# Down stages of a retention and SwiGLU kernel: both score groups of the first pair in one part, the second group in the banks of later token blocks

## The chip, the cores and the metric

The kernel runs on one core of a Trainium2 chip. The metric is the device time of one execution in microseconds, as a median of several runs. A profiled execution gives a trace as well, with a start and a duration for every instruction of the five engines: TensorE (PE, with its weight loads as PEld), VectorE (DVE), ScalarE (ACT), GpSimd (POOL) and SyncE (SP, which issues most DMAs here).

## The reference

Two blocks follow each other. The first is a recurrent retention over 4 batches, 8 heads, 768 tokens and a head size of 64:

```python
for t in range(S):
    state = gamma[None, :, None, None] * state + np.einsum('bhd,bhe->bhde', k[:, :, t], v[:, :, t])
    y[:, :, t] = scale * np.einsum('bhd,bhde->bhe', q[:, :, t], state)
```

Its output, as 3072 tokens of 512 features, goes through a SwiGLU feed-forward block with 1536 hidden features:

```python
g = x @ w_gate
silu = g * (1.0 / (1.0 + np.exp(-g)))
val = x @ w_val
return (silu * val @ w_out).astype(np.float32)
```

## The kernel before

**Tiling.** The sequence is cut into chunks of 128 tokens, six for each batch. Three chunks of one batch and the three of the same place in the next batch make a segment of 768 tokens, and four segments make the whole. A *pair* is the two chunks, one of each batch, at one place of a segment, so a segment has three pairs, 0 to 2.

**Stages.** For each segment there is an up stage, which makes the hidden features from the attention output, and a down stage, which multiplies them by `w_out`. The first segment's attention and up stage are written out by hand (`START`, `beside`, function `up`, line 695). The later up stages (`up3`, matmuls at line 866) split their operands into three terms. A down stage (line 916) goes over the 12 blocks of 128 hidden features; for each it runs six *token blocks* of 128 tokens, each three matmuls of 128x128 by 128x512, and each token block accumulates in a PSUM bank of its own, 0 to 5, over the whole stage. So a down stage has 72 slots, numbered n = 6f + b. The three terms of a hidden block are made by `h_split`: ScalarE (line 760), VectorE (line 763) and, for the third term, VectorE again (line 80).

**Attention inside a down stage.** The down stages of the first three segments also compute the attention of the next segment. It is cut into parts, which stand between token blocks at fixed slots. For each pair the parts are: scores of group 0, scores of group 1 (a group is four of the eight heads), "m" (own-half mix), "o" (other-half mix) and "t" (new states):

```python
CYCLE = [("s", 0, 0), ("s", 1, 4), ("m", 0, 9), ("o", 0, 12), ("t", 0, 16)]
STARTS = (2, 22, 41)
```

All matmuls of these parts are issued by the helper `mm` (line 551). They are small: they use a quarter of the array (64 by 64), or half of it for the states. The trace has 32 records of matmuls for one scores part, 16 with 128 columns and 16 with 64. `scores_of(p, g)` writes the two halves of a group's scores into banks 6 and 7 (`R0` is 6). `decayed` (line 570) then multiplies each half by its mask on VectorE and puts it into one of four places of `tmp`. `scale_q2` multiplies the pair's q in place by a decay (one chunk on VectorE, line 80, and one on GpSimd, line 624), where the next segment is not at the start of a sequence. It needs both groups' scores to have read q.

**Order of work.** Nothing is decided while the kernel runs. Every piece is put into a list with a planned time (`at(t, fn)`), the list is sorted by that time, and each engine and DMA queue gets its instructions in that order. The planned times (`WHEN`, `COST`, `PASS_D`) thus set only the order. Waits between engines are added by the framework from the tiles that instructions read and write. Each engine and queue works in order, so an instruction that waits holds those behind it.

**Around the change.** In the first down stage the last gate products of the up stage (`last_gates`, with results at lines 710 and 711) come after the first token block, and the first round of token blocks has its own order, (0, 4, 3, 2, 5, 1). In the others the order is 0 to 5. Ahead of the second and third down stage, `up3` uses banks 0 to 3, 6 and 7. SP's queue brings later pairs' k, q and v (`load_pair`, line 545) and the blocks of `w_out` (`w_load`, line 909), in planned order.

Of the kernel before, what the change touches and what calls it, by code (L numbers as in the profile page):

```python
# [17 lines left out]
P = 128  # L18
B, H, S, D = 4, 8, 768, 64
# [13 lines left out]
TA = 3 * P  # L33
# [16 lines left out]
def tile_retnet_swiglu(  # L50
# [22 lines left out]
    add, mul, sub = ALU.add, ALU.mult, ALU.subtract  # L73
    tt, stt, pool = (nc.vector.tensor_tensor, nc.vector.scalar_tensor_tensor,
                     nc.gpsimd.tensor_tensor)
# [39 lines left out]
    banks = [psum.tile([P, 512], F32, name=f"bank{i}") for i in range(8)]  # L115
# [4 lines left out]
    def at(t, fn, *args, **kw):  # L120
        events.append((t, len(events), lambda: fn(*args, **kw)))
# [23 lines left out]
    def seg_chunks(s):  # L145
        p, pos = divmod(s * L, NCK)
        return [(2 * p + i) * NCK + pos + j for j in range(L) for i in range(2)]
# [144 lines left out]
    def do(order):  # L292
# [40 lines left out]
    WHEN = {  # L333
        ('u', 0): (1.15, 2.16, 2.86, 3.39, 4.9, 5.3, 8.05, 13.63, 7.4, 8.1),
        ('u', 1): (0.41, 2.51, 3.16, 3.92, 4.38, 5.59, 6.95, 8.3, 7.26, 12.66),
        ('u', 2): (0.33, 1.32, 3.61, 3.15, 4.0, 5.51, 5.85, 6.13, 7.28, 7.66),
        ('u', 3): (1.63, 1.81, 3.34, 2.86, 3.53, 5.07, 6.18, 7.14, 7.05, 7.54),
        ('w', 0, 0): (-11.39, -6.27, -4.75),
        ('w', 0, 1): (-7.89, -7.84, -1.53),
        ('w', 0, 2): (-10.42, -10.31, -9.95),  # L340
        ('w', 1, 0): (-9.1, -4.79, -3.1),
# [71 lines left out]
    att = {}  # L413
    first_chunks = seg_chunks(0)

    def pairs(t):
        return t.rearrange("p (n t) -> p n t", n=NP)
# [84 lines left out]
    def mix(c):  # L502
        vn, a = chunks[c][2], att.pop(c)
        y, own = y_parts(c)
        for k, (n, i, to) in enumerate(own):
# [11 lines left out]
    side = [t.rearrange("p (i t) -> p i t", i=2)  # L517
            for t in (tab[:, : 2 * TA], kept_vk.rearrange("p a b -> p (a b)")[:, : 2 * TA])]
    kdec_b = tab[:, ds(2 * TA, H)]
    half = [ds(0, D), ds(D, D)]  # L520
    given = {}
    R0 = 6
# [27 lines left out]
    def mm(o, a, b, start=False):  # L550
        nc.tensor.matmul(o, a, b, start=start, stop=True, skip_group_check=True)  # L551

    def scores_of(p, g):
        kt, qt = ([pairs(t) for t in given[p][w]] for w in range(2))
        for b in range(2):
            for m in range(2):
                for r in range(2):
                    x, n = half[r], 2 * g + b
                    mm(banks[R0 + r][half[m], ts(b, P)], kt[m][x, n, half[0]],
                       qt[m][x, n], b == 0)  # L560
        for b in range(2):
            for m in range(2):
                for r in range(2):
                    x, n = half[r], 2 * g + b
                    mm(banks[R0 + r][half[m], ds(2 * P + D * b, D)],
                       kt[1 - m][x, n, half[1]], qt[1 - m][x, n, half[1]])

    def decayed(p, g, i):
        att[p, g, i] = tmp[:, ts(2 * g + i, TA)]
        tt(att[p, g, i], banks[R0 + i][:, :TA], side[g][:, i], op=mul)  # L570

    def y_both(h, i, c):
        return banks[R0 + c].rearrange("p (i b t) -> p i b t", i=2, b=2)[half[h], i]
# [245 lines left out]
    def make_x(t, s, p):  # L819
        for m, d in enumerate(WHEN["sum", p]):  # L820
            at(t + d, sum_x, m)
        for n in range(3):
            for d, step in zip(WHEN["far", p, n], (
                    lambda n=n: far_a(*x_part(s, p, n)), lambda n=n: far_b(*x_part(s, p, n)),
                    lambda n=n: far_c(x_part(s, p, n)[0]), lambda n=n: far_d(x_part(s, p, n)[0]))):
                at(t + d, step)
# [66 lines left out]
    def h_split(t, f, when):  # L893
        it = {}

        def begin():
            hs[f] = item("g", 2 * TH)
            it["o"] = [hs[f][:, i] for i in range(3)]
            near_a(it["o"], hT[:, f].rearrange("p i t -> p (i t)"))

        a, b, c = WHEN["h", when]
        at(t + a, begin)
        at(t + b, lambda: near_b(it["o"], hT[:, f].rearrange("p i t -> p (i t)")))
        at(t + c, lambda: near_c(it["o"], both))

    def w_load(t, f):
        def load():
            wo[f] = item("o", DM)
            nc.sync.dma_start(out=wo[f].bitcast(U32), in_=w_dn3[f])

        at(t - 8.0, load)
# [25 lines left out]
        nc.sync.dma_start(out=out[ds(row, P)], in_=t)  # L937


    CYCLE = [("s", 0, 0), ("s", 1, 4), ("m", 0, 9), ("o", 0, 12), ("t", 0, 16)]  # L940
    STARTS = (2, 22, 41)
    PARTS = {}
    for p, b in enumerate(STARTS):
        for what, g, n in CYCLE:
            PARTS[b + n] = what, p, g
    COST = {"s": 1.0, "m": 1.3, "o": 1.1, "t": 0.8}
    LOADS = {5: 7, 6: 15, 7: 19, 8: 19, 9: 27, 10: 39, 11: 46}
    UNITS = (40, 59, 62)

    def down_stage(s, t, first_order=range(6), between=None):  # L950
        nxt = s + 1 if s + 1 < NSEG else None
        slot_at, steps = [], []
        for n in range(6 * NF):
            f, b = divmod(n, 6)
            slot_at.append(t)
            if b == 0:
                steps.append(t)
            if nxt and n in PARTS:
                what, p, g = PARTS[n]
                ci = seg_chunks(nxt)[2 * p] % NCK  # L960
                d = t + COST[what] + 0.1
                if what == "s":
                    at(t, scores_of, p, g)
                    w = WHEN["s", p, g]
                    for i in range(2):
                        at(d + w[i], decayed, p, g, i)
                    if g and ci:
                        for i in range(2):
                            at(d + w[2 + i], scale_q2, p, i)
                elif what == "m":  # L970
                    at(t, mix_own, nxt, p)
                    w = WHEN["m", p]
                    at(d + w[0], fence)
                    if ci < NCK - 1:
                        for i in range(2):
                            at(d + w[1 + i], scale_k2, p, i)
                elif what == "o":
                    at(t, mix_other, nxt, p)
                    if p == 0:
                        at(t, begin_x, nxt)  # L980
                    for k, w in enumerate(WHEN["y", p]):
                        at(d + w, bring_y, k % 2, k // 2 % 2, k // 4)
                    if ci < NCK - 1:
                        at(d + WHEN["old", p], decay2, nxt, p)
                    make_x(d, nxt, p)
                elif ci < NCK - 1:
                    at(t, state2, nxt, p)
                    at(d + WHEN["new", p], keep_state, nxt, p)
                t += COST[what]
            tok = (first_order if f == 0 else range(6))[b]  # L990
            at(t, down, f, tok)
            t += 3 * PASS_D
            if f == NF - 1:
                at(t + WHEN["end" if nxt else "last"][tok], finish, s, tok)
            if between and n == 0:
                at(t, between)
                t += 1.0
        for f in range(NF):
            h_split(steps[f], f, f if nxt else NF)
            if s or f > 2:  # L1000
                w_load(steps[f], f)
        if nxt:
            for n, h in LOADS.items():
                at(slot_at[h] + 1.0, load_pair, nxt, n)
            for f in range(3):
                at(slot_at[UNITS[f]], load_unit, f)
        return t
# [24 lines left out]
    end = T0 + NF * UP0  # L1032
# [4 lines left out]
    at(end, do, beside[-1])  # L1037
    for n in range(3, 5):
        at(end + 1.0 + n, load_pair, 1, n)
    t = down_stage(0, end, (0, 4, 3, 2, 5, 1), last_gates)  # L1040
    for s in range(1, NSEG):
        for f in range(NF):
            up3(s, f, t + UPT * f)
            if f > 2:
                at(t + UPT * (f - 1) - 2.5, load_unit, f)
        t += NF * UPT
        if s + 1 < NSEG:
            for n in range(5):
                at(t - (18, 13, 12, 5, 4)[n], load_pair, s + 1, n)
        t = down_stage(s, t)  # L1050
# [52 lines left out]
```

## Time and profile before

| | |
|---|---|
| median of 3 runs | 669.22 us (667.5 to 669.8) |
| profiled execution | 669.52 us |
| its span, first to last instruction | 667.7 us |
| TensorE busy | 655.4 us, 98% of the span |
| VectorE, ScalarE, GpSimd busy | 463.1, 386.2, 252.0 us |
| granted TensorE clock | 1.000 |
| chain that ended last | 82% TensorE, 8% DMA, 3% VectorE |

Rows of the timeline give the start in us, the duration of the group in us, engine, line, operation, what it writes and reads, the shape, the count, and in brackets how long the engine had been idle and what ended the idle time. "issue" there means that no wait on another engine is recorded. Rows of the chain of waits give start, duration and what was on the chain. PE records overlap their neighbours a little, and their ends are modelled, so the chain, which has no overlaps, is the better ruler for TensorE.

### The profile page before, as it was taken

The numbers are of one execution on the slowest core, as the hardware profiler recorded it, in microseconds if no ns is written. First come the engines' busy times: TensorE is split into PE (matmuls) and PEld (weight loads), VectorE is DVE, ScalarE is ACT, GpSimd is POOL, SyncE is SP. The second block draws the span as 40 slices with busy tenths as digits, with TensorE's granted clock in tenths as the row PEclk, the third lists the DMA queues.
The fourth block names the chain that finished last, engine by engine and source line by source line (L and its number), as shares of the span: only waits on it lengthen the run. The fifth ranks groups of instructions, "written<-read, shape, count | busy, mean of one in ns | idle before, by whom it ended". The sixth has DMA issues, their size and how long they took to land.

```text
span 667.7 us, 12348 instructions
## 1 busy us (share of the span) xinstructions
PE 655.4 (98%) x4712; PEld 547.5 (82%) x4712; DVE 463.1 (69%) x742; ACT 386.2 (58%) x792; POOL 252.0 (38%) x165
## 2 busy tenths in 40 slices
PE   8998999999999999999999999999999999999997
PEld 7754555567778999997777999998777999999885
DVE  3667988887778767675778666667766776668541
ACT  2687887755737555555648655555574655654111
POOL 1444657730104655640111655661000656652000
PEclk9999999999999999999999999999999999999999
DMA  8799799877665533455674534365766444323553
GB/s 325 268 388 340 250 402 393 334 261 237 226 214 218 197 110 129 169 176 206 238 251 168 206 111 145 112 210 180 240 216 228 161 177 151 111 89 110 188 189 142
DMA packets 48459, 141.32 MB, mean 212 GB/s; under 512 B 4752, under 2 KB 17808, under 8 KB 48400
## 3 DMA queue, kind: packets, MB, share of 16 engines
q1 hardware_dynamic: 47968, 139.88, 59.7%
q8 instruction: 37, 0.61, 0.4%
q10 hardware_dynamic: 432, 0.66, 0.3%
q14 instruction: 22, 0.18, 0.1%
HBM read 113.78 MB, written 26.74 MB: 210 GB/s over the span
## 4 chain that ended last, share of the span: by engine, by line
PE 82%; DMA 8%; DVE 3%; ACT 2%; issue 2%; SPq 1%; POOL 1%; ACTq 0%; POOLq 0%; DVEq 0%
PE bank L866 39%; PE bank L916 29%; PE bank L695 6%; PE bank L551 6%; DMA rawp<-in_w_gate_dram 2%; DMA loads<-in_w_out_dram 1%; DMA oitem<-wdnt 1%; DMA tab<-in_decays_dram 1%; DMA wdnt<-oitem 1%; SPq L194 1%; DMA hT<-in_q_t_dram 1%; POOL first L237 1%; ACT bank L221 1%; DVE first L231 0%; ACT chunk_x L801 0%
## 5 line engine op out<-in xcount | busy, mean ns | idle before, releaser
L866 PE MATMUL bank<-x,gitem 128*128 128x384 f32 x1296 | 231.5, 335 | 0.0
L866 PEld LDWEIGHTS bank<-x,gitem 128*128 128x128 f32 x1296 | 226.0, 188 | 0.5
L916 PE MATMUL bank<-oitem,gitem 128*128 128x512 f32 x864 | 215.1, 401 | 0.6 <-DMA oitem<-wdnt 0.4
L916 PEld LDWEIGHTS bank<-oitem,gitem 128*128 128x128 f32 x864 | 158.7, 188 | 41.5 <-issue 2.9
L766 POOL TENSOR_TENSOR gitem<-gitem 128x768 fp32r<-128x768 f32 x72 | 138.5, 1946 | 114.7 <-DVE gitem L763 110.3
L695 PE MATMUL bank<-first 128*128 128x384 f32 x336 | 110.8, 489 | 2.8 <-ACT tmp L716 1.4
L695 PEld LDWEIGHTS bank<-first 128*128 128x128 f32 x336 | 62.9, 190 | 48.8 <-ACT tmp L732 2.6
L760 ACT ACTIVATE gitem<-loads 128x768 fp32r<-128x768 f32 x72 | 58.1, 841 | 36.3 <-issue 29.4
L624 POOL TENSOR_TENSOR loads<-loads,tab 128x512 f32<-128x512 f32 x8 | 12.7, 1584 | 143.2 <-PE bank L551 143.2
L763 DVE SCALAR_TENSOR_TENSOR gitem<-gitem,loads 128x768 fp32r<-128x768 f32 x72 | 65.8, 954 | 0.0
L760 ACT ACTIVATE gitem<-hT 128x768 fp32r<-128x768 f32 x48 | 40.1, 839 | 36.7 <-PE bank L916 24.5
L763 DVE SCALAR_TENSOR_TENSOR gitem<-gitem,hT 128x768 fp32r<-128x768 f32 x48 | 45.8, 960 | 18.1 <-ACT gitem L760 18.0
L237 POOL TENSOR_TENSOR first<-first,rawp 128x1024 int32<-128x1024 int32 (+1 forms) x21 | 40.8, 1953 | 31.0 <-DVE first L231 14.5
L80 DVE SCALAR_TENSOR_TENSOR gitem<-gitem 128x768 fp32r<-128x768 f32 x48 | 46.0, 964 | 0.8
L801 ACT COPY chunk_x<-bank 64x256 f32<-64x256 f32 x72 | 25.5, 367 | 34.0 <-PE bank L551 33.3
L882 ACT COPY tmp<-bank 128x384 f32<-128x384 f32 x36 | 17.3, 479 | 46.1 <-PE bank L866 42.9
L866 PE MATMUL bank<-x,oitem 128*128 128x384 f32 x216 | 43.8, 338 | 0.0
L766 POOL TENSOR_TENSOR oitem<-oitem 128x256 fp32r<-128x256 f32 x36 | 28.3, 786 | 30.0 <-DVE oitem L763 28.0
L885 DVE TENSOR_TENSOR hT<-hT,bank 128x384 f32<-128x384 f32 x36 | 19.9, 553 | 27.2 <-ACT bank L885 27.2
L883 DVE TENSOR_TENSOR hT<-bank,tmp 128x384 f32<-128x384 f32 x36 | 20.1, 557 | 26.6 <-PE bank L866 26.6
L866 PEld LDWEIGHTS bank<-x,oitem 128*128 128x128 f32 x216 | 38.1, 188 | 0.0
L881 DVE TENSOR_TENSOR tmp<-bank,tmp 128x384 f32<-128x384 f32 x36 | 20.0, 557 | 19.1 <-PE bank L866 19.1
(99 smaller groups left out, 723.8 us busy)
## 6 DMA issues: line engine op xcount, KB each, us to landing
oitem<-wdnt SPq DMA_DIRECT2D x45, 768.0 KB, 4.4
loads<-wup SPq DMA_DIRECT2D x36, 896.0 KB, 4.8
wup<-first SPq DMA_DIRECT2D x12, 896.0 KB, 8.8
wdnt<-oitem SPq DMA_DIRECT2D x12, 768.0 KB, 4.7
rawp<-in_w_gate_dram SPq DMA_DIRECT2D x12, 512.0 KB, 7.7
rawp<-in_w_val_dram SPq DMA_DIRECT2D x12, 512.0 KB, 7.5
out_dram<-chunk_x SPq DMA_DIRECT2D x23, 256.0 KB, 2.3
loads<-in_q_t_dram SPq DMA_DIRECT2D x18, 256.0 KB, 3.9
```

The lines of the kernel that those rows point to most:

```text
L80: stt(o, x, 1.0, y, op0=mul, op1=op)
L237: pool(d.bitcast(I32), d.bitcast(I32), lo.bitcast(I32), op=add)
L551: nc.tensor.matmul(o, a, b, start=start, stop=True, skip_group_check=True)
L695: nc.tensor.matmul(o, w[:, slot, k], a[:, KH - 1 - k], start=(start and k == 0), stop=(stop and k == KH - 1), skip_group_check=True)
L760: act(o[0], x, AF.Copy, scale=CUT / FAR)
L763: stt(o[1], f32(o[0]), -FAR, x, op0=mul, op1=add)
L766: op(o[2], f32(o[0]), f32(o[1]), op=add)
L801: copy(cx[half[i], ds(2 * h, 2), c], y_both(h, i, c))
L866: nc.tensor.matmul(o, w[:, a, k], xs_of[s][:, a, OP[p], KH - 1 - k], start=start and a == k == 0, stop=a == 2 and k == KH - 1, skip_group_ ...
L881: steps = (lambda: copy(p1, x), lambda: tt(c11, z, p1, op=add), lambda: act(gate, c11, AF.Silu, scale=ONE), lambda: copy(u2, x), lambda: c ...
L883: lambda: copy(p5, wb), lambda: tt(h1, x, p5, op=add),
L916: nc.tensor.matmul(banks[tok], hs[f][:, a, ds(i * TH + u * P, P)], wo[f][:, a], start=f == a == 0, stop=f == NF - 1 and a == 2, skip_group ...
```

## The change

For pair 0, and for that pair only, the scores of both groups are one part at slot 2 of the down stage. The part at slot 6 is deleted. Group 1 is issued first. It takes two other banks, which a new argument of `scores_of` names: 4 and 5, or 4 and 3 in the first down stage. `decayed` finds a group's banks in the new table `score_banks`. The masks of group 1 are planned ahead of those of group 0. `scale_q2` for that pair moves with them. The planned start of the second hidden block is taken one part's cost earlier than the part's end, which leaves the planned times of its pieces as they were. The first round of token blocks in the first down stage is now in the order (0, 2, 5, 1, 4, 3), in which banks 4 and 3 come last.

On VectorE's queue this gives four masks in a row in each of the three stages, ahead of line 80's piece for the second hidden block; where q is scaled, line 80's scaling of q now stands ahead of line 763 for the third hidden block. The order on ScalarE, GpSimd and SP is the same as before. The number of instructions is the same on every engine.

```diff
--- before.py
+++ after.py
@@ -550,24 +550,27 @@
     def mm(o, a, b, start=False):
         nc.tensor.matmul(o, a, b, start=start, stop=True, skip_group_check=True)
 
-    def scores_of(p, g):
+    score_banks = {}
+
+    def scores_of(p, g, own=(R0, R0 + 1)):
+        score_banks[p, g] = own = [banks[i] for i in own]
         kt, qt = ([pairs(t) for t in given[p][w]] for w in range(2))
         for b in range(2):
             for m in range(2):
                 for r in range(2):
                     x, n = half[r], 2 * g + b
-                    mm(banks[R0 + r][half[m], ts(b, P)], kt[m][x, n, half[0]],
+                    mm(own[r][half[m], ts(b, P)], kt[m][x, n, half[0]],
                        qt[m][x, n], b == 0)
         for b in range(2):
             for m in range(2):
                 for r in range(2):
                     x, n = half[r], 2 * g + b
-                    mm(banks[R0 + r][half[m], ds(2 * P + D * b, D)],
+                    mm(own[r][half[m], ds(2 * P + D * b, D)],
                        kt[1 - m][x, n, half[1]], qt[1 - m][x, n, half[1]])
 
     def decayed(p, g, i):
         att[p, g, i] = tmp[:, ts(2 * g + i, TA)]
-        tt(att[p, g, i], banks[R0 + i][:, :TA], side[g][:, i], op=mul)
+        tt(att[p, g, i], score_banks[p, g][i][:, :TA], side[g][:, i], op=mul)
 
     def y_both(h, i, c):
         return banks[R0 + c].rearrange("p (i b t) -> p i b t", i=2, b=2)[half[h], i]
@@ -937,12 +940,14 @@
         nc.sync.dma_start(out=out[ds(row, P)], in_=t)
 
 
+
     CYCLE = [("s", 0, 0), ("s", 1, 4), ("m", 0, 9), ("o", 0, 12), ("t", 0, 16)]
     STARTS = (2, 22, 41)
     PARTS = {}
     for p, b in enumerate(STARTS):
         for what, g, n in CYCLE:
             PARTS[b + n] = what, p, g
+    del PARTS[STARTS[0] + 4]
     COST = {"s": 1.0, "m": 1.3, "o": 1.1, "t": 0.8}
     LOADS = {5: 7, 6: 15, 7: 19, 8: 19, 9: 27, 10: 39, 11: 46}
     UNITS = (40, 59, 62)
@@ -954,17 +959,24 @@
             f, b = divmod(n, 6)
             slot_at.append(t)
             if b == 0:
-                steps.append(t)
+                steps.append(t - COST["s"] if nxt and f == 1 else t)
             if nxt and n in PARTS:
                 what, p, g = PARTS[n]
                 ci = seg_chunks(nxt)[2 * p] % NCK
                 d = t + COST[what] + 0.1
                 if what == "s":
+                    if p == 0:
+                        at(t, scores_of, 0, 1, (4, 5) if s else (4, 3))
+                        d += COST["s"]
+                        t += COST["s"]
+                        for i in range(2):
+                            at(d + 0.1 * i, decayed, 0, 1, i)
                     at(t, scores_of, p, g)
-                    w = WHEN["s", p, g]
+                    w = WHEN["s", p, g] if p else (0.2, 0.3)
                     for i in range(2):
                         at(d + w[i], decayed, p, g, i)
-                    if g and ci:
+                    if (g or p == 0) and ci:
+                        w = WHEN["s", p, 1]
                         for i in range(2):
                             at(d + w[2 + i], scale_q2, p, i)
                 elif what == "m":
@@ -1037,7 +1049,7 @@
     at(end, do, beside[-1])
     for n in range(3, 5):
         at(end + 1.0 + n, load_pair, 1, n)
-    t = down_stage(0, end, (0, 4, 3, 2, 5, 1), last_gates)
+    t = down_stage(0, end, (0, 2, 5, 1, 4, 3), last_gates)
     for s in range(1, NSEG):
         for f in range(NF):
             up3(s, f, t + UPT * f)
```

## The prediction

> **What bounds the kernel now.** I read the busy shares first, then the chain of waits in order of time around the three down stages that the change touches, then the timelines of VectorE, ScalarE and the DMA queue at the same places.
>
> ```profile
> PE 655.4 (98%) x4712; PEld 547.5 (82%) x4712; DVE 463.1 (69%) x742; ACT 386.2 (58%) x792; POOL 252.0 (38%) x165
> ...
> PE bank L866 39%; PE bank L916 29%; PE bank L695 6%; PE bank L551 6%; DMA rawp<-in_w_gate_dram 2%; DMA loads<-in_w_out_dram 1%; DMA oitem<-wdnt 1%; DMA tab<-in_decays_dram 1%; DMA wdnt<-oitem 1%; SPq L194 1%; DMA hT<-in_q_t_dram 1%; POOL first L237 1%; ACT bank L221 1%; DVE first L231 0%; ACT chunk_x L801 0%
> ```
>
> TensorE sets the time; the small attention matmuls of line 551 hold 6% of the chain. What matters is how the chain runs at the start of a down stage. This is the second one (start us, us, what; L916 are token blocks, three matmuls each; L551 are attention parts):
>
> ```profile
> 299.40 1.40 PE bank L916 x6
> 300.80 0.83 PE bank L551 x32
> 301.63 3.00 PE bank L916 x12
> 304.63 0.83 PE bank L551 x32
> 305.46 3.70 PE bank L916 x15
> 309.16 1.03 PE bank L551 x32
> 310.19 2.30 PE bank L916 x9
> 312.50 0.62 PE bank L551 x32
> ```
>
> The two 0.83 us pieces are the scores of groups 0 and 1 of the first pair. There is no wait on another engine between 299.40 and 312.50; what is not arithmetic here is the price of going in and out of a part. It comes from differences of these rows. Token matmuls: 9, 12 and 15 take 2.30, 3.00 and 3.70, so three more cost 0.70 (0.233 each) and each stretch after a part carries a fixed 2.30 - 9 x 0.233 = 0.20 us. Parts: a part of 48 (first and third down stage, 1.47 us, the 16 more with N=128) against the 32 with N=128 here (1.03) gives 0.44 for 16 with N=128, so 32 cost 0.88 and the part's fixed price is 0.15; 32 with N=64 (0.62) less 0.15 leaves 0.47, or 0.235 for 16. A scores part is 16 + 16: 0.15 + 0.44 + 0.235 = 0.825, and the row says 0.83.
>
> **The change part by part.** *One part instead of two.* Before: two parts and the two fixed prices behind them, 2 x (0.83 + 0.20) = 2.06. After: 0.15 + 2 x 0.675 + 0.20 = 1.70. Saved: 0.35 us per stage (0.15 in, 0.20 out), all of it on TensorE, which is the chain. The weight loads show the same boundary from the other side, an idle of 0.37 us at every entry that waits for nothing recorded:
>
> ```profile
> 304.56 0.76 PEld L551 LDWEIGHTS bank<-loads 64*64 64x64 f32 x32 [0.37 <-issue]
> ```
>
> Bounds for it: 0.15 if only the entry goes, 0.37 if the whole idle of the row above goes. I take 0.35, from the four differences that agree.
>
> *A longer part.* No part of before has 64 matmul records in a row, the longest has 48. [...] By the row, the last 16 records of the 48-long part cost 0.44 us, 27 ns each. [...]
>
> *Where the second group's banks go.* Group 1 now sits in banks 4 and 5 (4 and 3 in the first down stage), and the token blocks 4 and 5 (4 and 3) write those banks next. They now wait for VectorE's masks at line 570. VectorE in the second down stage:
>
> ```profile
> 299.94 0.56 DVE L885 TENSOR_TENSOR hT<-hT,bank 128x384 f32<-128x384 f32 x1 [0.41 <-ACT bank L885]
> 301.70 1.02 DVE L570 TENSOR_TENSOR tmp<-bank,tab 128x384 f32<-128x384 f32 x2 [1.20 <-PE bank L551]
> 302.64 0.95 DVE L80 SCALAR_TENSOR_TENSOR gitem<-gitem 128x768 fp32r<-128x768 f32 x1
> 305.53 1.02 DVE L570 TENSOR_TENSOR tmp<-bank,kept_vk 128x384 f32<-128x384 f32 x2 [1.95 <-PE bank L551]
> ```
>
> VectorE is idle 1.20 us ahead of the first masks. After: TensorE computes group 1 first, done at 301.63 as group 0 was; its two masks run 301.70 to 302.72 and bank 4 is free near 302.25. TensorE ends group 0 at 300.80 + 0.15 + 1.35 = 302.30, passes blocks 2 and 3 (0.20 + 2 x 0.70) and reaches block 4 at 303.9, block 5 at 304.6: margins of 1.6 and 1.9 us. No stall. The third stage has the same rows 156.8 us later. In the first one VectorE is later because of the last gate products:
>
> ```profile
> 145.70 0.55 DVE L711 TENSOR_TENSOR hT<-bank,hT 128x384 f32<-128x384 f32 x1
> 146.17 1.01 DVE L570 TENSOR_TENSOR tmp<-bank,tab 128x384 f32<-128x384 f32 x2
> 147.10 0.95 DVE L80 SCALAR_TENSOR_TENSOR gitem<-gitem 128x768 fp32r<-128x768 f32 x1
> ```
>
> There the part runs 144.98 to 146.48. Blocks follow in the new order 5, 1, 4, 3: block 5 at 146.7 (bank 5 last read by line 710, before 145.8), block 1 at 147.4 (bank 1: line 711, 146.25), block 4 at 148.1 (mask done 146.7), block 3 at 148.8 (147.2). Smallest margin 0.9 us. Block 2, moved ahead of the part, needs bank 2, read last by line 735 over 3 us earlier. The order of the blocks costs nothing by itself.
>
> *What is queued behind the masks.* Two masks more (0.94 us) now stand ahead of line 80's piece of the second hidden block (third term, 302.64 before). The group 0 masks start at 302.64, after both 302.30 and the first two, so line 80 runs 303.58 to 304.53. TensorE starts that block at 302.30 + 3.00 = 305.30 and reads the third term two matmuls later, 305.77: margin 1.2 us. In the first stage: line 80 ends at 148.98, the term is read at 149.95, margin 1.0. Without this cover each microsecond late is one on the chain, three times.
>
> *Moved earlier.* The masks of group 1 leave 305.53, so line 763 behind them waits for ScalarE alone. ScalarE's line 760 there waits for the last read of the first hidden block, and that comes later, since all 64 score records are now ahead of it:
>
> ```profile
> 304.72 0.84 ACT L760 ACTIVATE gitem<-hT 128x768 fp32r<-128x768 f32 x1 [3.33 <-issue]
> ```
>
> and SP's queue:
>
> ```profile
> 306.38 5.07 SPq L909 DMA_DIRECT2D oitem<-wdnt  x2
> ```
>
> Its release moves from 304.63 to 305.30, so line 760 ends near 306.2 and line 763 starts about then, not later than its 306.47 of before. The copies of line 635 behind it (3.92 us) end at 310.1 and ScalarE has nothing until 313. The scaling of q (VectorE 0.68 us, GpSimd 1.29 us, first and third stage) moves ahead of line 763, into the time in which that waits for ScalarE; GpSimd idles 10 us before it. SP's queue holds pair 1's q loads (305.52 before) until group 1's scores have read the old q; they go near 302.4 now, and the load of w_out that follows can start when its slot is free, at 305.4 instead of 306.38. All hidden: worth nothing, and no loss.
>
> **The sum.** 3 x 0.35 = 1.05 us. The profiled execution took 669.52 us (span 667.7, 1.8 around it), so 668.5; against the median of 669.22, 668.2. That is 0.16%, less than the 0.3% that a measurement of this kernel can tell from no change.
>
> **The rivals.**
> *The gain is spent at a later wait.* TensorE idles 0.64 us at 355.94 (line 551, on copies of line 801) and 0.37 us at 485.91 (on a load of w_out). If these don't move with TensorE they swallow up to 0.35 each: 668.9. For it: they are there. Against: the copies wait for TensorE's own mix part, and SP's queue for its reads, so both come earlier too.
> *Slower: matmul supply.* The place is records 33 to 64 of the joined part. If they cost over 0.675 + 0.35 = 1.03 us, 32 ns each, the change loses. [...] Against: 27 ns in the row.
> *A larger gain.* SP's queue freed 3 us earlier may remove the two waits above, 1.0 us: 667.2. For: SP stands behind reads of TensorE for long. Against: the second load waits for later blocks either way.
>
> **How the numbers follow.** Forecast 0.70, spent later 0.12, supply 0.10, larger gain 0.08. Three runs spread over 2.3 us, so a median carries some 0.7 us; the forecast's own range is 667.2 to 669.2. The range over the cases: 666.9, with the larger gain inside, to 670.6, which leaves out the upper half of the supply case. Faster by over 0.3% (below 667.2): a tenth of the forecast, most of the larger gain, some scatter, 0.18. Slower by over 0.3% (above 671.2): the upper end of the supply case and a wait I haven't seen, 0.09. Within: 0.73.
>
> **What would show it.** In the chain: one piece of the attention line (551, three lines further down after the change) with 64 records near 1.50 us (over 1.86 speaks for supply), then 27 token matmuls without a break in 27 x 0.233 + 0.20 = 6.50. On VectorE four masks in a row, 1.9 us, and no idle of TensorE that ends with line 570 or line 80. The up stages begin 0.35, 0.7 and 1.05 us earlier. It is wrong if a token block in banks 3, 4 or 5 waits for a mask, if the second hidden block waits for its third term, or if the joined part is longer.

## The result

The changed kernel takes 667.29 us (median of 20 runs), the kernel before 669.38 us in the same comparison (20 runs). The ratio is 0.9969, with a 95% interval of 0.9957 to 0.9980: 2.1 us less, between 1.3 and 2.9. The forecast was 668.2 us and 1.05 us less than before.

The profiled executions are further apart than the medians, 665.43 us (span 663.6) against 669.52 us (span 667.7). The page of the kernel after gives the same picture of what bounds it (busy us, share of the span, instructions):

```profile
PE 652.2 (98%) x4712; PEld 546.0 (82%) x4712; DVE 463.1 (70%) x742; ACT 386.2 (58%) x792; POOL 252.3 (38%) x165
```

The chain of waits of the kernel after, at the start of the second down stage (start us, us, what; the token matmuls are now line 919):

```profile
297.73 1.40 PE bank L919 x6
299.13 1.50 PE bank L551 x64
300.63 6.50 PE bank L919 x27
307.13 1.03 PE bank L551 x32
308.16 2.30 PE bank L919 x9
310.46 0.62 PE bank L551 x32
```

One piece of 64 records stands where two of 32 stood. It takes 1.50 us, and the 27 token matmuls behind it take 6.50, that is 27 x 0.233 + 0.20. Before, the same work from the first scores to the mix part took 309.16 - 300.80 = 8.36 us; now it takes 307.13 - 299.13 = 8.00. That is 0.36 us less, and the two other stages show the same pieces, 1.50 and 6.49 or 6.50. The weight loads of the kernel after have the idle of an entry only once for both groups:

```profile
299.06 1.43 PEld L551 LDWEIGHTS bank<-loads 64*64 64x64 f32 x64 [0.36 <-issue]
```

VectorE in the timeline of the kernel after, same place:

```profile
298.27 0.55 DVE L888 TENSOR_TENSOR hT<-hT,bank 128x384 f32<-128x384 f32 x1 [0.41 <-ACT bank L888]
300.01 1.02 DVE L573 TENSOR_TENSOR tmp<-bank,kept_vk 128x384 f32<-128x384 f32 x2 [1.18 <-PE bank L551]
300.95 1.01 DVE L573 TENSOR_TENSOR tmp<-bank,tab 128x384 f32<-128x384 f32 x2
301.88 0.95 DVE L80 SCALAR_TENSOR_TENSOR gitem<-gitem 128x768 fp32r<-128x768 f32 x1
302.74 0.95 DVE L766 SCALAR_TENSOR_TENSOR gitem<-gitem,hT 128x768 fp32r<-128x768 f32 x1
```

Four masks stand in a row and the piece of line 80 ends at 302.83, before TensorE starts that hidden block at 303.6. No token block waits for a mask.

What the two profiled executions differ by, from their chains (us; a stage runs from its first piece to the next stage's first piece):

| Stretch | before | after | difference |
|---|---|---|---|
| start to first token block | 142.29 | 141.09 | -1.20 |
| to the first scores | 2.69 | 2.69 | 0.00 |
| first scores to first later up stage | 66.50 | 66.14 | -0.36 |
| up stage | 87.92 | 87.81 | -0.11 |
| second down stage | 69.04 | 68.15 | -0.89 |
| up stage | 87.79 | 87.78 | -0.01 |
| third down stage | 68.52 | 67.54 | -0.98 |
| up stage | 88.87 | 88.78 | -0.09 |
| last down stage and end of the span | 54.08 | 53.62 | -0.46 |

Three times 0.35 is the joined part. The rest is elsewhere. In the second down stage an idle of 0.64 us ahead of the third pair's new states is 0.13 us. In the third an idle of 0.37 us for a load of `w_out` is gone, and with it the slower token block behind that idle (0.94 us for its three matmuls in place of 0.70). The stretch up to the first token block, which the change doesn't touch, was 1.20 us shorter. The last row is the end of the kernel. Its chain has a write of the output that takes 2.33 us before and 2.08 after:

```profile
661.53 2.33 DMA out_dram<-chunk_x
...
657.90 2.08 DMA out_dram<-chunk_x
```

The experiments ask which of this belongs to the change.

### The profile page after: what moved, and what is told of

Its sections match the earlier page's. It is cut to its first block, busy times and chain, and to the rows that moved or that the text cites. A ratio compares the mean times of both kernels' runs of the same rounds, so it can differ in the third digit from the quotient of the medians.

```text
span 663.6 us, 12350 instructions
## 1 busy us (share of the span) xinstructions
PE 652.2 (98%) x4712; PEld 546.0 (82%) x4712; DVE 463.1 (70%) x742; ACT 386.2 (58%) x792; POOL 252.3 (38%) x165
## 4 chain that ended last, share of the span: by engine, by line
PE 84%; DMA 8%; DVE 2%; ACT 2%; issue 1%; SPq 1%; POOL 1%; ACTq 0%; POOLq 0%; DVEq 0%
PE bank L869 39%; PE bank L919 31%; PE bank L551 7%; PE bank L698 7%; DMA rawp<-in_w_gate_dram 2%; DMA loads<-in_w_out_dram 1%; DMA hT<-in_v_n_dram 1%; DMA wdnt<-oitem 1%; SPq L194 1%; DMA rawp<-in_w_out_dram 1%; DMA hT<-in_k_n_dram 1%; DMA hT<-in_k_t_dram 1%; POOL first L237 1%; ACT rawp L224 0%; ACT bank L221 0%
```

## The experiments

Three explanations were to be told apart. *Price of a part:* going into and out of an attention part costs TensorE 0.35 us, and that is the gain. *Freed queue:* reading the scores 3 us earlier releases SP's queue and shrinks the two later waits; this was the mechanism of the prediction's rival with the larger gain. *Chance:* the two waits vary with the time that DMAs take, whatever the kernel.

**One stage, or two, joined.** The joining is made to depend on the stage (parts of the edit to the changed kernel):

```diff
-    del PARTS[STARTS[0] + 4]
+    JOINED = (0,)
...
-            if nxt and n in PARTS:
+            if nxt and n in PARTS and not (s in JOINED and n == STARTS[0] + 4):
...
-                    if p == 0:
+                    if p == 0 and s in JOINED:
```

> One part instead of two in the first down stage alone; the second and third as before. Price-of-a-part theory: the joined part takes 1.50 us and is followed by token matmuls at 0.233 us each plus 0.20, the stage is 0.35 us shorter than before, and nothing else moves: -0.35 us. Freed-queue theory (the rest of the gain comes from later waits that shrink because the scores are read earlier): the same here, since the first stage had no such wait; the second and third stage keep their waits of 0.64 us (attention part before the third pair's new states) and 0.37 us (a load of w_out). Chance theory (those two waits come and go with the time that DMAs take): they may be larger or smaller in this run although nothing there is changed.

Measured: 0.9988 of before (0.9977 to 1.0000), 0.8 us less with an interval of 1.5 to 0.0. The first down stage has 1.50 and 6.50 in its chain. The second and third are as before, but their waits are not: 0.40 us in place of 0.64, and none in place of 0.37.

```profile
144.22 1.50 PE bank L551 x64
145.72 6.50 PE bank L919 x27
...
299.48 0.83 PE bank L551 x32
...
354.57 0.40 issue
```

The same with `JOINED = (1, 2)` and the old block order in the first stage:

> One part in the second and third down stage alone, the first as before. Price-of-a-part theory: -0.7 us. Freed-queue theory: -0.7 and about -0.9 more from the two waits, which are gone or near 0.13 us as in the profile after the change, so -1.6 us. Chance theory: the waits vary, the mean is -0.7 us.

Measured: 0.9972 (0.9960 to 0.9983), 1.9 us less, between 1.1 and 2.7. The wait ahead of the new states is 0.12 us; a wait on a load of `w_out` is back, this time in the second stage (0.5 us, at 328.0). So the waits move between kernels in which nothing near them was changed. The time is nearer to 1.6 than to 0.7, and this run alone would speak for the freed queue. (Part of it is a shorter end of the kernel, which the section on the prediction comes to.)

**Both groups early, but in two parts.** Group 1 keeps its new banks and its early place; one token block stands between the groups.

```diff
+    PARTS[2], PARTS[3] = ("e", 0, 1), ("s", 0, 0)
...
-                if what == "s":
-                    if p == 0:
-                        at(t, scores_of, 0, 1, (4, 5) if s else (4, 3))
+                if what == "e":
+                    at(t, scores_of, 0, 1, (4, 5) if s else (4, 3))
```

> Group 1 first and in the later banks, as in the changed kernel, but one token block stands between the two groups, so there are two parts again, both early; masks in the changed order. Price-of-a-part theory: the 0.35 us of each of three stages comes back, two parts of 0.83 us, and the time is that of before (0.0 against before, +1.05 against the changed kernel). Freed-queue theory: the scores are still read some 3 us earlier than before, so the further 0.9 us of gain stay: -0.9 to -1.0 us against before. No token block waits for a mask in either.

Measured: 1.0005 (0.9990 to 1.0020). No gain is left to be seen, and the wait ahead of the new states is 0.43 us. The scores are still read early: the second part ends 2.55 us after the first begins (302.47 - 299.92), where it was 4.66 before and 1.50 in the joined part. The chain of this kernel has each part's price in the open:

```profile
299.92 0.83 PE bank L551 x32
300.75 0.89 PE bank L919 x3
301.64 0.83 PE bank L551 x32
302.47 5.79 PE bank L919 x24
```

Three token matmuls between two parts take 0.89 us in place of 0.70, and 24 take 24 x 0.233 + 0.20. This speaks against the freed queue: 0.9 to 1.0 us less would have been outside the interval of -0.7 to +1.3 us. As the scores are read 2.1 us earlier here, not the 3 us of the expectation, it does not exclude an effect that needs the last microsecond.

**More parts.** In a first version, all scores parts of the kernel before were cut in two:

```diff
-    CYCLE = [("s", 0, 0), ("s", 1, 4), ("m", 0, 9), ("o", 0, 12), ("t", 0, 16)]
+    CYCLE = [("a", 0, 0), ("s", 0, 1), ("a", 1, 3), ("s", 1, 4), ("m", 0, 9), ("o", 0, 12), ("t", 0, 16)]
```

> The kernel before with every scores part of all three pairs cut in two at the border between its 128-column and its 64-column matmuls, a token block between the halves: the same matmuls in 18 parts more. Price-of-a-part theory: 18 x 0.35 = +6.3 us, the halves 0.15 + 0.44 = 0.59 and 0.15 + 0.235 = 0.385 us long. If the price at the border is only how the trace models the ends of matmuls: 0 us. Anything over 6.3 us would be masks that come later.

Measured: 1.016 (1.014 to 1.0181), 10.7 us more. In this kernel one of the two masks of the first pair's group 0 was planned ahead of the second half of its scores, so that mask was taken from incomplete scores. The pieces are as expected, 0.60 and 0.39 us, but the cut also moved masks and the pieces of hidden blocks: TensorE waits for line 886's result at the end of two up stages (1.5 us), and near 170 and 490 us for late masks, which end at 170.73 and 490.95 in the chain, with the next scores at 170.77 and 490.99. The time can't be read as the price of a part. A second version cuts the first pair only and places all its masks behind the second halves:

```diff
+    PARTS[2], PARTS[3], PARTS[5], PARTS[6] = ("a", 0, 0), ("s", 0, 0), ("a", 0, 1), ("s", 0, 1)
...
-                if what == "s":
-                    at(t, scores_of, p, g)
+                if what == "a":
+                    at(t, scores_a, p, g)
+                elif what == "s":
+                    at(t, scores_of if p else scores_b, p, g)
```

> The kernel before with the four halves of the first pair's scores (128-column and 64-column matmuls of each group) in four parts instead of two, a token block between the halves, and the masks after the second halves: six parts more in the whole kernel. Price-of-a-part theory: +6 x 0.35 = +2.1 us, halves of 0.59 and 0.385 us in the chain. If the price at the borders is only how the trace models the ends of matmuls: 0.

Measured: 1.0069 (1.0053 to 1.0085), 4.6 us more, between 3.5 and 5.7. The chain:

```profile
301.84 0.60 PE bank L551 x16
302.44 0.90 PE bank L923 x3
303.34 0.39 PE bank L551 x16
303.73 1.59 PE bank L923 x6
305.32 0.60 PE bank L551 x16
305.92 0.90 PE bank L923 x3
306.81 0.39 PE bank L551 x16
307.20 3.69 PE bank L923 x15
```

and its waits of TensorE (line and releaser: us in total, times, longest):

```profile
PE bank L873 <- DVE hT L890: 1.5, 2, 0.7
```

Each half and each stretch carries its 0.15 and 0.20: the six parts more account for 2.1 us. Another 1.5 us is a side effect. The planned costs of the parts also shift the split of a hidden block, and its VectorE piece (line 770, 297.64 to 298.60 in the chain) now stands directly ahead of line 890, for which the last matmuls of the up stage wait. That makes 3.6, at the lower end of the interval. Without the side effect, 2.0 to 4.2 us remain where 0 was expected if the price were an artefact of modelled ends. It is thus real, as far as no further side effect is hidden in this run, which doesn't measure it to better than a microsecond.

**A part of 128 records.** For the supply rival, in which the later records of a long part cost more (at over 32 ns each the second group's would undo the gain), both groups' scores are computed twice in the joined part:

```diff
+                    if p == 0:
+                        at(t, scores_of, p, g)
+                        at(t, scores_of, 0, 1, (4, 5) if s else (4, 3))
                     at(t, scores_of, p, g)
```

> The changed kernel with both groups' scores of the first pair computed twice over in the joined part (128 matmul records in a row, the second time over the same results). Price-of-a-part theory: 0.15 + 4 x 0.675 = 2.85 us for the part, since 128- and 64-column records go on at 27 and 15 ns each however long the part is. [...]

Measured, in all three stages:

```profile
301.83 2.84 PE bank L551 x128
304.67 6.49 PE bank L919 x27
```

2.84 us against 2.85 worked out. The records after the 64th cost what the first did, 21 ns each as a mean of both widths ((2.84 - 1.50) / 64). The supply rival is refuted for every length that the change has.

**Banks that the next block takes.** How near is the wait that the change avoids? Group 0 goes into banks 2 and 3:

```diff
-                    at(t, scores_of, p, g)
+                    at(t, scores_of, p, g, (2, 3) if p == 0 and s else (R0, R0 + 1))
```

> The changed kernel, but in the second and third down stage group 0 goes into banks 2 and 3, which the very next token blocks write, instead of 6 and 7; group 1 stays in 4 and 5 and is masked first. By the prediction's working for banks (a pair of masks ends 0.94 us after it starts, four masks stand in a row): masks 1 and 2 run from 0.90 to 1.84 us after the part's start, mask 3 ends near 2.40, and TensorE wants bank 2 at 1.50 to 1.70, so the first token block behind the part waits 0.7 to 0.9 us in each of the two stages and the following ones don't: about +0.45 us against before in all. If waits for banks are hidden anyway: no idle of TensorE, as in the changed kernel.

Here the masks of group 0 stayed planned behind the token block that takes bank 2, so the first of them was taken from that block's product instead of the scores, and the order of waiting was another one than the expectation describes. TensorE did one token block, then waited 1.1 us for two masks in each stage. A second version also plans the masks of that pair earlier:

```diff
-                            at(d + 0.1 * i, decayed, 0, 1, i)
+                            at(d + 0.1 * i - (1.0 if s else 0.0), decayed, 0, 1, i)
...
-                    w = WHEN["s", p, g] if p else (0.2, 0.3)
+                    w = WHEN["s", p, g] if p else ((-0.7, -0.6) if s else (0.2, 0.3))
```

> As the run with group 0 in banks 2 and 3, but with the masks planned ahead of the token blocks that take these banks, so that the results are the same as before and TensorE has to wait for the masks. Masks 1 and 2 run from 0.90 to 1.84 us after the part's start, masks 3 and 4 end near 2.35 and 2.80; TensorE ends the part at 1.50 and wants bank 2 at once: it waits 0.7 to 0.9 us there in the second and in the third down stage. Block 3 follows 0.70 later and waits no more. In the first down stage, unchanged, no wait. If a bank's wait were hidden, no idle.

Measured (timeline of TensorE, second down stage; the third has the same):

```profile
299.13 1.57 PE L551 MATMUL bank<-loads 64*64 64x128 f32 x64
301.62 2.60 PE L919 MATMUL bank<-oitem,gitem 128*128 128x512 f32 x10 [0.92 <-DVE tmp L573]
```

0.92 us of idle, twice, where 0.7 to 0.9 had been worked out, and none behind it. The working for the margins in banks 4 and 5 rests on the same durations of masks, so this wait, where it was expected, speaks for those margins.

**How the waits vary.** The two kernels were profiled again unchanged:

> The kernel before, unchanged, to see how its waits differ from one execution to the next. Chance theory: the wait ahead of the third pair's new states in the second down stage, 0.64 us in the first profile of it and 0.40 and 0.43 in the two kernels that keep two parts there, and the wait on a load of w_out in the third, 0.37 us and 0 in those, come out at other values again, 0.1 to 0.7 and 0 to 0.5. Theory that joining shortens the first wait: it is 0.40 or more here.

> The changed kernel, unchanged, for the same. Both theories have the joined parts at 1.50 us and 27 token matmuls at 6.50 behind them. Chance theory: the wait ahead of the third pair's new states in the second down stage is anywhere between 0.1 and 0.7. Theory that joining shortens it: 0.12 to 0.13 again.

The wait ahead of the new states in the second down stage was 0.13 us in the kernel before and 1.18 us in the changed one, the reverse of the first pair of profiles. The second wait was absent in both. Over all executions with this order on ScalarE, the first wait was:

| second down stage | wait in us |
|---|---|
| two parts or more (6 profiles) | 0.64, 0.13, 0.40, 0.43, 0.62, 1.27 |
| one joined part (6 profiles) | 0.13, 1.18, 0.12, 0.56, 0.62, 1.26 |

The means are 0.58 and 0.65, and both rows range from about 0.1 to 1.3. The difference of 0.51 us in the first two profiles is thus no effect of the change that these profiles can show. Where the wait comes from is seen in the changed kernel's second profile, chain first, ScalarE's timeline after it:

```profile
351.87 1.06 PE bank L551 x48
352.93 2.99 PE bank L919 x12
355.92 1.18 issue
```

```profile
350.36 2.02 ACT L638 ACTIVATE loads<-loads,tab 128x64 f32<-128x64 f32 x8 [8.69 <-DMA loads<-in_k_n_dram]
352.29 0.83 ACT L763 ACTIVATE gitem<-hT 128x768 fp32r<-128x768 f32 x1
353.02 1.05 ACT L784 ACTIVATE x<-x 128x1024 fp32r<-128x1024 f32 x1
354.08 2.92 ACT L804 COPY chunk_x<-bank 64x256 f32<-64x256 f32 x8
```

The mix part ends at 352.93, but ScalarE copies its result only from 354.08: it had waited for a DMA with k until 350.36 and had three more groups of instructions ahead of the copies. TensorE needs the copies done before it may write the new states into that bank: they end at 357.00, and the new states begin at 357.10. To test this, the scaling of line 784 (781 before) was moved behind the copies, in the kernel before:

```diff
-        ('far', 1, 0): (4.92, 6.5, 9.67, 16.37),
+        ('far', 1, 0): (4.92, 6.5, 9.67, 23.0),
```

> The kernel before, with one ScalarE instruction of each down stage moved: the last scaling of the second pair's x (1.05 us, four of 128x8x128) now stands behind the copies of the third pair's output instead of ahead of them. If the wait ahead of the third pair's new states is those copies starting late behind that scaling, it falls from 0.4 to 0.64 to about 0.12, its floor (the eight copies take 2.93 us plus some 0.2 of signals, the four token blocks meanwhile 3.00). If something else holds it, it stays at 0.4 to 0.64. The two scores parts stay at 0.83 us.

```profile
354.86 0.13 issue
```

0.13 us, as expected of the cause. But a wait of 0.12 or 0.13 also came up in 3 of 12 executions without the move, so this profile alone proves little. The same move in the changed kernel:

> The changed kernel with ScalarE's last scaling of the second pair's x behind the copies of the third pair's output, as in the run that moved it in the kernel before. The wait ahead of the third pair's new states in the second down stage is 0.12 to 0.13 us in every execution, where the changed kernel showed 0.13 and 1.18. Against before: -1.05 us for the parts and some -0.4 us (its mean of four executions with the scaling ahead, less the floor), -1.4 us; if the moved scaling is late for the next up stage or is in the way there, no better than the changed kernel.

Measured: the wait is 0.12 us again, and the time is 0.9979 of before (0.9966 to 0.9992), 1.4 us less with an interval of 0.5 to 2.3. That is the expected number, but the chain shows that the other case of the expectation came true as well: at the start of the first later up stage the chain now leaves TensorE and passes over GpSimd (in the changed kernel and in the one before, the chain has no stop there).

```profile
207.03 3.89 POOL gitem L769
...
210.97 87.29 PE bank L869 x500
```

From the first scores to the start of the last up stage, less the wait ahead of the new states, this kernel takes 377.73 us (521.88 - 144.03 - 0.12), and the changed kernel 377.29 and 377.22. So its chain without that wait is 0.4 to 0.5 us longer, and part of what the move wins is lost again. Its time cannot be told from the changed kernel's own 2.1 (1.3 to 2.9), and no better version is claimed.

## Why the prediction was right, and what of it was not

*The sum.* Its one term, 0.35 us for each stage, is confirmed by the chain. From the start of the first scores to the start of the last up stage, less the wait ahead of the new states, five profiles without a wait for `w_out` give 378.37 (before again: 524.34 - 145.84 - 0.13) and 378.29 us with two parts in every stage (before again, two near), 377.84 with the first stage joined, 377.29 and 377.22 with all three (after, after again). The joined kernels are 1.07 us shorter, where 1.05 had been forecast, and one stage gives 0.49.

*The time.* The measured 2.1 us is twice that, and its interval ends at 1.3. The range held it, but the gain was forecast too small: the joined parts are shown to give about half of it, so that the forecast's own number is not confirmed by the time. The wait ahead of the new states is no shorter on average with the change (table above). The start of the program is not either: up to the first token block it takes 141.9 us as a mean of five profiles with two parts in every stage (141.05 to 143.15) and 142.0 of six with all three stages joined (141.09 to 143.16).

One further part of the gain is in every profile, and the sum put it at nothing: the end of the kernel, from the last down stage's first token block to the end of the span.

| kernels | last down stage and end, us | the output write in the chain, us |
|---|---|---|
| two parts in the second and third stage, group 1 in banks 6 and 7 (6 profiles) | 54.05 to 54.16 | 2.33 to 2.37, once 2.56 |
| group 1 in banks 4 and 5 there, joined or near (8 profiles) | 53.62 to 53.73 | 2.06 to 2.09 |

The two ranges don't meet, and the means are 0.4 us apart. The 201 token matmuls of that stage take 47.17 to 47.19 us in all of them, so the difference is in writing the output. The kernel with two parts near to each other has it too, so it doesn't come from joining. Why the writes land sooner is open, for no run changes only that. With it the sum is 1.05 + 0.4, about 1.5 us, inside the interval of 1.3 to 2.9. The other timed comparisons allow the same sum: 0.8 (0.0 to 1.5) for 0.35 with the first stage joined, 1.9 (1.1 to 2.7) for 1.1 with the two later ones, -0.3 (-1.3 to 0.7) for 0.4 with two near parts, and 1.4 (0.5 to 2.3) for the changed kernel with the scaling moved. What is left, about 0.6 us of the median, is not told from chance by these runs; the waits for `w_out`, which are in some profiles of both kinds, may be part of it.

*The rivals.* That the gain is spent at a later wait is not seen: the waits come and go in kernels of both kinds, and the chain without them keeps the whole 1.07 us. The slower supply is refuted by the part of 128 records: 2.84 us, 21 ns a record, as in the part of 64 (1.50 us). No run shows the slower supply on which the upper end of the range, 670.6, the chance of 0.10 and part of the 0.09 rest; the joined part took the 1.50 us worked out for it in every stage. The larger gain has a time (667.2) that fits the median best, but its mechanism is not borne out: with the queue freed early and two parts, no gain was measured. The first wait is no shorter on average with the change, and the second is absent in the kernel before's second profile too.

*The margins.* TensorE ended the joined part 1.50 us after its start, line 80 ran where it was put (301.88, against 301.91 worked out with the stage 1.67 us earlier), and no mask held a block. One reading was wrong without cost: line 766 (763 before), which stands behind line 80, was said to wait for ScalarE's line 763 (760 before). It ran at 302.74, before that one began:

```profile
303.71 0.85 ACT L763 ACTIVATE gitem<-hT 128x768 fp32r<-128x768 f32 x1 [3.99 <-issue]
```

It works on a first term that ScalarE had made long before (two runs of line 763 from 298.15 to 299.72). The release of ScalarE's line 763 itself moved as described, to the last read of the first hidden block: 303.71, against 303.63 worked out.

## What to carry to other kernels

Where small tiled matmuls are cut into a stream of full-array ones, count the borders: differences between stretches of different length, read from the chain, give the fixed price (here 0.15 us in and 0.20 us out), and bringing two parts together was worth just that on the chain (0.36 us in each stage), provided the banks can be borrowed. A borrowed bank came free when VectorE had got through its queue up to that bank's mask: with group 0 in banks 2 and 3, the third of the four masks ended at 301.58, and TensorE went on at 301.62. That time could be worked out from durations before: banks wanted two token blocks later cost no wait, banks wanted by the very next token block cost 0.92 us. A wait that differs between two single profiles is no evidence for a change until the same kernel has been profiled again. And compare every stretch over all profiles, those that the change doesn't touch as well: here the end of the kernel, which no edit names, holds a steady 0.4 us.

## What the runs showed that was not expected

The wait ahead of the new states ranges from 0.12 to 1.27 us over twelve executions of kernels with the same order of instructions around it. In the profile examined its length follows the landing of one DMA, through three groups of ScalarE instructions that happen to be queued ahead of the copies. Together with a start of the program that took 141.09 us in one execution and 143.15 or 143.16 us in two others, one of each kernel, this is as large as the gain of the change.
